# Scores of the first two batches with q as the stationary operand, in a TensorE-bound attention and gated-FFN kernel

## The chip, the cores and the metric

The kernel runs on one core of one Trainium2 chip. The metric is the device time of one execution in microseconds (us), the median of several runs. The engines are TensorE (PE: matmuls; its weight loads are shown as PEld), VectorE (DVE), ScalarE (ACT), GpSimd (POOL) and SyncE (SP, whose queue issues most of the transfers).

## The reference

```python
# q, k, v: (8 batches, 8 heads, 576 tokens, 64);  phi: (8, 8, 576, 32)
a = softmax(phi, over the 576 tokens)               # per memory slot
k_m = a.T @ k;  v_m = a.T @ v                       # 32 memory slots per head
attn = softmax(q @ k_m.T / 8, over the 32 slots)    # 576 x 32 per head
x = attn @ v_m                                      # heads side by side: 4608 x 512
out = (sigmoid(x @ w_gate) * (x @ w_val)) @ w_out   # 512 -> 1536 -> 512
```

All arrays are float32 to the caller. The weights come to the kernel in a form that it must convert to float32 on the chip.

## The kernel before, in words

The kernel never forms x. For each batch it multiplies v_m with the gate and value weights first (U: 32 slots of 8 heads by 256 columns for each of 12 blocks f of d_ff), and then U with the attention weights. Both operands are split into a high part and a rest (`at_hi`, `at_lo`, `u_hi`, `u_lo`), and each product is made of three matmuls (hi x hi, hi x lo, lo x hi). The same is done for the output product with `wo_hi`, `wo_lo`, `g_hi`, `g_lo`.

A step is one batch b and one block f, in two halves c of the tokens (0: the first 256; 1: the other 320, `CUT`). The first 20 steps, with all attention of batches 0 to 3 and part of batch 4's and all that is loaded and converted for them, are not planned by a loop but written out as a fixed list, `OPENING`. Each entry is an action; the entries of the list are issued in its order, so that on PE, DVE and ACT every engine works through its entries in that order, and on SP's queue the transfers stand in that order too. An engine whose next entry is not ready waits, whatever stands behind it. After the list, a loop does the other steps; it is not touched.

The actions that matter here (b is the batch, c the half of the tokens; for batches 2 and 3 mx, ms and hi, lo take both halves at once):

- `phi b`, `kvt b`, `kvm b g`, `q b c`, `gate f`, `out f`: transfers in. `more`, `keep`, `again`, `row`, `fetch`: further transfers (weights, spilled attention weights, partial outputs). The tiles ph, kvt, kvm0, kvm1 and q exist once each, so the next batch's transfer waits until the last reader is done.
- `sz`, `bc`, `bt` (gate weights) and `ws`, `wc`, `wb`, `wh`, `wl` (output weights): conversion, on ACT and DVE.
- `amax`, `aexp`, `T`, `A`, `Z`: the first softmax; T are PE transposes, A their copies out of PSUM. `K b g`, `B`, `t`, `V`: k_m and v_m, turned and kept.
- `S b c`: the scores. The 32 slots of a head are the stationary operand (64 rows x 32 columns), q is the moving one (`scores_of`), so slots lie on the partitions. `tr`: DVE transposes them in blocks of 32x32 out of PSUM into the tile e, tokens on partitions. `mx`, `ms`, `ex`, `nz`, `nm`: maximum, subtraction, exponential, sum and its reciprocal, product. `tn`: DVE transposes back. `hi`, `lo`: `at_hi` on ACT and `at_lo` on DVE.
- `U b f`: U for blocks f and f + 1 into two PSUM banks. `uh`: `u_hi` on ACT. `ul`: `u_lo`, on DVE the bank less `u_hi`. For (0, 0) and (0, 2), listed in `BY_PE`, `um` first has PE put minus `u_hi` into the banks and add the same sum once more, so that the bank holds the rest, and `ul` is a copy on ACT (`u_minus`, `u_rest`).
- `G b f c`: the 12 matmuls of gate and value; `sg`, `gm`, `gh`, `gl`: sigmoid, product and its split. `O b f c`: the six output matmuls; `E`, `row`: a partial or final row out.
- `W n`: n matmuls whose result nobody reads, put where PE would otherwise have nothing to do; another 24 stand ahead of the list.

PSUM has eight banks; until the first O, seven of them are handed out in turn (`bank`), and a bank is handed out again when its last reader is done.

Of the kernel before, what the change touches and what calls it, by code (L numbers as in the profile page):

```python
# [64 lines left out]
hi 1; gl 0 2 0; lo 1; O 0 2 0; sg 0 3 1; gh 0 2 1; gm 0 3 0; G 1 0 0; q 2 1; gm 0 3 1; gh 0 3 0; q 2 0;
gl 0 2 1; ws 3; kvm 3 0; gl 0 3 0; gh 0 3 1; keep 0; wc 3; G 1 0 1; sg 1 0 0; gl 0 3 1; sz 4; gm 1 0 0;
wb 3; sg 1 0 1; G 1 1 0; gh 1 0 0; amax 3; wh 3; O 0 2 1; sg 1 1 0; gm 1 0 1; gm 1 1 0; wl 3; S 2 0;
S 2 1; aexp 3; tr 2 0; O 0 3 0; tr 2 1; gl 1 0 0; mx 2; U 1 2; E 0 3 0 0; G 1 1 1; uh 1 2; ms 2;
E 0 3 0 1; gh 1 0 1; ul 1 2; O 0 3 1; row 0 3 1; row 0 3 0; ex 2; kvt 3; gl 1 0 1; G 1 2 0; more 1;
nz 2; O 1 0 0; sg 1 1 1; gh 1 1 0; gm 1 1 1; E 0 3 1 0; nm 2; G 1 2 1; E 0 3 1 1; sg 1 2 0; row 0 3 3;  # L70
gl 1 1 0; gm 1 2 0; O 1 0 1; bc 4; sg 1 2 1; gh 1 1 1; gm 1 2 1; U 2 0; tn 2; G 1 3 0; uh 2 0;
gl 1 1 1; hi 2; ul 2 0; O 1 1 0; gh 1 2 0; lo 2; gh 1 2 1; G 1 3 1; sg 1 3 0; sz 5; gl 1 2 1; q 3 1;
gm 1 3 0; q 3 0; gl 1 2 0; T 3 1; keep 1; Z 3; T 3 2; sg 1 3 1; O 1 1 1; A 3 1; gm 1 3 1; bc 5; T 3 0;
G 2 0 0; A 3 0; phi 4; row 0 3 2; A 3 2; gh 1 3 0; K 3 0; sg 2 0 0; gh 1 3 1; gm 2 0 0; gl 1 3 0; bt 4;
K 3 1; G 2 0 1; B 3; more 2; t 3; sg 2 0 1; G 2 1 0; V 3 0; gm 2 0 1; V 3 1; bt 5; O 1 2 0; S 3 0;
gh 2 0 0; gl 1 3 1; O 1 2 1; sg 2 1 0; tr 3 0; more 3; gm 2 1 0; gl 2 0 0; S 3 1; gh 2 0 1; U 2 2;
sz 6; tr 3 1; O 1 3 0; mx 3; uh 2 2; G 2 1 1; ul 2 2; E 1 3 0 0; gh 2 1 0; row 1 3 0; E 1 3 0 1; ms 3;
row 1 3 1; O 1 3 1; sg 2 1 1; keep 2; gm 2 1 1; gl 2 0 1; G 2 2 0; bc 6; ex 3; O 2 0 0; gl 2 1 0;
E 1 3 1 0; nz 3; E 1 3 1 1; G 2 2 1; gh 2 1 1; gl 2 1 1; nm 3; O 2 0 1; sg 2 2 0; sg 2 2 1; gm 2 2 0;
gm 2 2 1; G 2 3 0; tn 3; O 2 1 0; sg 2 3 0; ws 4; gm 2 3 0; amax 4; gh 2 2 0; G 2 3 1; gh 2 2 1; hi 3;  # L80
wc 4; gl 2 2 0; U 3 0; gh 2 3 0; gl 2 2 1; sg 2 3 1; gm 2 3 1; O 2 1 1; uh 3 0; lo 3; U 3 2; gl 2 3 0;
keep 3; ul 3 0; row 1 3 2; O 2 2 0; uh 3 2; row 1 3 3; ul 3 2; G 3 0 0; aexp 4; bt 6; O 2 2 1;
gh 2 3 1; G 3 0 1; more 4; O 2 3 0; sg 3 0 0; gm 3 0 0; wb 4; gh 3 0 0; G 3 1 0; E 2 3 0 0; sg 3 0 1;
row 2 3 0; gm 3 0 1; T 4 1; gl 2 3 1; G 3 1 1; A 4 1; sg 3 1 0; E 2 3 0 1; gm 3 1 0; gl 3 0 0;
gh 3 0 1; row 2 3 1; O 2 3 1; more 5; sg 3 1 1; kvm 4 1; gm 3 1 1; again 0; gl 3 0 1; U 0 4; E 2 3 1 0;
gh 3 1 0; G 3 2 0; uh 0 4; sz 7; ul 0 4; O 3 0 0; gh 3 1 1; bc 7; G 3 2 1; wh 4; E 2 3 1 1; wl 4;
sg 3 2 0; gm 3 2 0; O 3 0 1; gl 3 1 0; sg 3 2 1; gh 3 2 0; gm 3 2 1; G 3 3 0; ws 5; gh 3 2 1; gl 3 2 1;
O 3 1 0; gl 3 1 1; gl 3 2 0; sg 3 3 0; wc 5; G 3 3 1; wb 5; O 3 1 1; gm 3 3 0; sg 3 3 1; bt 7; wh 5;
gh 3 3 0; G 0 4 0; O 3 2 0; gl 3 3 0; more 6; sg 0 4 0; Z 4; kvm 4 0; gm 3 3 1; row 2 3 2; gm 0 4 0;
G 0 4 1; row 2 3 3; O 3 2 1; sg 0 4 1; gh 3 3 1; gm 0 4 1; more 7; U 0 6; G 0 5 0; uh 0 6; ul 0 6;  # L90
O 3 3 0; gl 3 3 1; G 0 5 1; wl 5; sg 0 5 0; gh 0 4 0; ws 6; E 3 3 0 0; wc 6; O 3 3 1; E 3 3 0 1;
row 3 3 0; gm 0 5 0; wb 6; row 3 3 1; G 0 6 0; gl 0 4 0; more 8; sg 0 5 1; O 0 4 0; gh 0 4 1; gm 0 5 1;
E 3 3 1 0; G 0 6 1; gh 0 5 0; E 3 3 1 1; gl 0 5 0; gl 0 4 1; gh 0 5 1; row 3 3 3; row 3 3 2; sg 0 6 0;
gl 0 5 1; O 0 4 1; wh 6; kvt 4; gm 0 6 0; sg 0 6 1; wl 6; gh 0 6 0; G 0 7 0; gm 0 6 1; ws 7; gl 0 6 0;
wc 7; O 0 5 0; sg 0 7 0; fetch 0 0; wb 7; gh 0 6 1; again 1; U 1 4; gl 0 6 1; wh 7; gm 0 7 0; O 0 5 1;
gh 0 7 0; sz 8; gl 0 7 0; wl 7; fetch 0 1; T 4 2; uh 1 4; O 0 6 0; ul 1 4; T 4 0; O 0 6 1; A 4 0;
A 4 2; O 0 7 0; G 0 7 1; E 0 7 0 0; E 0 7 0 1; row 0 7 0; row 0 7 1; K 4 0; sg 0 7 1; gm 0 7 1;
gh 0 7 1; K 4 1; gl 0 7 1; bc 8; fetch 0 2; U 1 6; B 4; uh 1 6; t 4; bt 8; O 0 7 1; V 4 0; V 4 1;
fetch 0 3; ul 1 6; E 0 7 1 0; E 0 7 1 1; row 0 7 3; row 0 7 2;
# [402 lines left out]

# [599 lines left out]
```

## Time and profile before

| | |
|---|---|
| median of 3 runs | 735.59 us (735.53 to 737.86) |
| the profiled execution | 736.14 us, span of its instructions 734.4 us |
| mean granted TensorE clock | 0.999 |
| PE busy | 724.2 us (99%), 5693 matmul records |
| PE weight loads busy | 607.7 us (83%) |
| DVE busy | 421.0 us (57%) |
| ACT busy | 337.6 us (46%) |
| DMA | 93.15 MB, mean 127 GB/s |

Times in the profile are microseconds from the span's first instruction. Busy time of PE includes the filler matmuls, and the end of a matmul is modelled: a matmul is shown for the whole of its way through the array, so that records overlap and the distance between the starts of two records tells the rate. A float32 matmul shows as two records, a transpose or a matmul of the split parts as one. A timeline row gives start, duration, engine, line of the kernel, operation, output and inputs, shape, how many records are merged in it (x), and in brackets how long the engine had been idle and what ended that. "64*32" is the part of the array in use, rows by columns; "64x256" is the moving operand.

### The profile page before, as it was taken

How to read it: one execution, taken by the hardware profiler on the slowest of the kernel's cores; microseconds unless marked ns; L12 is line 12 of the kernel's file. 1: busy time of each engine (PE TensorE's matmuls, PEld its weight loads, DVE VectorE, ACT ScalarE, POOL GpSimd, SP SyncE). 2: the span in 40 equal slices, each digit the busy share in tenths (PEclk: the TensorE clock that was granted, in tenths of full speed). 3: DMA queues.
4: the chain of work that ended last, by engine and by line, in shares of the span. 5: the costliest groups of instructions: out<-in, count | busy, mean ns of one | idle time of the engine just before them, and what ended most of it. 6: DMA issues, size and time to landing. Idle time of an engine off the chain costs nothing.

```text
span 734.4 us, 13802 instructions
## 1 busy us (share of the span) xinstructions
PE 724.2 (99%) x5693; PEld 607.7 (83%) x5693; DVE 421.0 (57%) x780; ACT 337.6 (46%) x787; POOL 4.5 (1%) x13
## 2 busy tenths in 40 slices
...
GB/s 364 358 285 195 207 279 168 237 172 226 273 342 160 243 150 80 132 165 15 148 238 58 2 94 147 29 30 65 1 1 59 1 0 15 1 58 1 1 1 71
DMA packets 29501, 93.15 MB, mean 127 GB/s; under 512 B 3328, under 2 KB 4352, under 8 KB 25856
## 3 DMA queue, kind: packets, MB, share of 16 engines
...
## 4 chain that ended last, share of the span: by engine, by line
PE 94%; DMA 4%; DVE 1%; SPq 0%; ACT 0%; issue 0%; POOL 0%; POOLq 0%; DVEq 0%; ACTq 0%
PE pu_t L186 55%; PE acc L186 39%; DMA kvm<-in_kvm_dram 2%; DMA q<-in_qT_dram 2%; DMA row<-part 1%; SPq L172 0%; DVE row L762 0%; DVE wg L280 0%; DVE e L509 0%; DVE e L524 0%; DVE mx L518 0%; DVE wo_raw L815 0%; ACT e L161 0%; ACT wo_raw L267 0%; ACT u_hi L627 0%
## 5 line engine op out<-in xcount | busy, mean ns | idle before, releaser
L186 PE MATMUL pu_t<-at_hi,u_hi 128*128 128x256 f32 (+1 forms) x764 | 227.7, 298 | 0.0
L186 PE MATMUL pu_t<-at_lo,u_hi 128*128 128x256 f32 (+1 forms) x764 | 224.4, 294 | 0.0
L186 PE MATMUL pu_t<-at_hi,u_lo 128*128 128x256 f32 (+1 forms) x764 | 224.0, 293 | 0.0
L711 DVE TENSOR_TENSOR sg<-pu_t,sg 128x256 f32<-128x256 f32 (+1 forms) x191 | 86.6, 455 | 160.2 <-ACT sg L161 98.3
L161 ACT ACTIVATE sg<-pu_t 128x256 f32<-128x256 f32 (+1 forms) x191 | 78.6, 412 | 194.7 <-PE pu_t L186 183.0
L186 PE MATMUL acc<-wo_hi,g_hi 128*128 128x512 f32 x384 | 154.6, 403 | 0.3 <-DVE row L762 0.3
L186 PEld LDWEIGHTS pu_t<-at_hi,u_hi 128*128 128x128 f32 x764 | 143.4, 188 | 11.7 <-issue 4.8
L186 PE MATMUL acc<-wo_hi,g_lo 128*128 128x512 f32 x384 | 151.1, 393 | 0.0
L186 PE MATMUL acc<-wo_lo,g_hi 128*128 128x512 f32 x384 | 150.6, 392 | 0.0
L186 PEld LDWEIGHTS pu_t<-at_lo,u_hi 128*128 128x128 f32 x764 | 143.4, 188 | 5.5
L186 PEld LDWEIGHTS pu_t<-at_hi,u_lo 128*128 128x128 f32 x764 | 143.2, 187 | 0.0
L722 ACT CAST g_hi<-sg 128x256 fp32r<-128x256 f32 x192 | 77.7, 406 | 109.0 <-DVE sg L711 96.3
L176 DVE TENSOR_TENSOR g_lo<-sg,g_hi 128x256 fp32r<-128x256 f32 x192 | 80.3, 420 | 61.8 <-ACT g_hi L722 61.7
L186 PEld LDWEIGHTS acc<-wo_hi,g_hi 128*128 128x128 f32 x384 | 72.0, 187 | 29.6 <-issue 19.0
L186 PEld LDWEIGHTS acc<-wo_hi,g_lo 128*128 128x128 f32 x384 | 72.1, 188 | 17.1
L186 PEld LDWEIGHTS acc<-wo_lo,g_hi 128*128 128x128 f32 x384 | 72.1, 188 | 9.4
L176 DVE TENSOR_TENSOR u_lo<-pu_t,u_hi 128x512 fp32r<-128x512 f32 x92 | 57.6, 684 | 27.5 <-ACT u_hi L627 27.5
L627 ACT CAST u_hi<-pu_t 128x512 fp32r<-128x512 f32 x95 | 49.4, 598 | 30.3 <-PE pu_t L186 30.0
L186 PE MATMUL pu_t<-wg,vT 64*32 64x512 f32 x784 | 50.8, 597 | 0.0
L186 PEld LDWEIGHTS pu_t<-wg,vT 64*32 64x32 f32 x784 | 11.9, 105 | 19.4 <-issue 17.0
L762 DVE TENSOR_TENSOR row<-acc,row 128x512 f32<-128x512 f32 x32 | 21.8, 688 | 6.8 <-DMA row<-part 3.7
L161 ACT ACT_TABLE_LOAD x18 | 23.1, 1283 | 1.0 <-PEq L1092 0.7
...
## 6 DMA issues: line engine op xcount, KB each, us to landing
...
```

What stands on the lines that cost most here:

```text
L161: last_act[0] = nc.scalar.activation(*args, **kw)
L176: return nc.vector.tensor_tensor(lo, x, hi.bitcast(F32), op=ALU.subtract)
L186: last_pe[0] = do(*args, **kw)
L627: nc.scalar.copy(U[b, fs[0]][0][:, r, :nf], pb[r])
L711: last_prod[0] = nc.vector.tensor_tensor(sg, val, sg, op=ALU.mult)
L722: nc.scalar.copy(ghi, prod[:, : 2 * P])
L762: nc.vector.tensor_tensor(st, o, st, op=ALU.add)
```

## The change

- The scores of batches 0 and 1 (`FLAT`) are made by `scores_flat`: q is the stationary operand (64 rows x 128 tokens), the 32 slots are the moving one. The result has tokens on the partitions at once, 256 columns to a bank, and a third bank takes the last 64 tokens of two heads' rows one under the other (`TAIL`).
- `tr` falls away for these batches. `flat_max` and `flat_minus` read the PSUM banks piece by piece (two pieces for c = 0, three for c = 1), and `flat_minus` writes e. For batch 1 they are done in two halves, too.
- `tn` is replaced by `tp`: PE turns the weights back, four transposes for c = 0 and five for c = 1, into PSUM; `hi` and `lo` read them there (`flat_hi`, `flat_lo`).
- `um`, `u_minus` and `u_rest` are gone; `ul` is DVE's subtraction everywhere. The tiles `minus` and `halves` are gone.
- The list `OPENING` is a new one, with the same actions otherwise. Some of what moved: phi 0 is first on SP's queue; kvm 1 0 and kvm 1 1 come after phi 2; K 1 0 and K 1 1 come after G 0 0 0; U 0 0 comes after tp 0 0; q 2 1 is ahead of kvm 2 1; kvm 4 1 comes late, after fetch 0 1; W 32 and W 16 stand around K 0 0.

```diff
+FLAT_CUT = {0: slice(0, 512), 1: slice(512, 2 * S), None: slice(0, 2 * S)}
...
+FLAT = (0, 1)
...
-BY_PE = [(0, 0), (0, 2)]
 OPENING = """
-out 0; gate 0; phi 0; kvt 0; gate 1; kvm 0 0; kvm 0 1; q 0 0; ws 0; wc 0; sz 0 0; sz 0 1; amax 0;
-bc 0 0; wb 0; aexp 0; bt 0 0; wh 0; W 65; T 0 0; bc 0 1; T 0 2; sz 1; T 0 1; wl 0; phi 1; A 0 2; q 0 1;
-bc 1; A 0 0; gate 3; A 0 1; W 14; K 0 0; Z 0; bt 1; kvm 1 0; W 3; K 0 1; B 0; bt 0 1; W 8; t 0; amax 1;
-V 0 0; V 0 1; W 4; S 0 0; tr 0 0; aexp 1; W 2; S 0 1; mx 0 0; U 0 0; ms 0 0; T 1 0; tr 0 1; ex 0 0;
-T 1 2; T 1 1; uh 0 0; nz 0 0; phi 2; kvt 1; sz 3; kvm 1 1; W 8; um 0 0; mx 0 1; gate 2; nm 0 0; out 1;
-A 1 2; q 1 0; A 1 1; ms 0 1; out 2; Z 1; q 1 1; ex 0 1; tn 0 0; nz 0 1; hi 0 0; A 1 0; amax 2; ul 0 0;
-W 27; K 1 0; nm 0 1; aexp 2; K 1 1; lo 0 0; tn 0 1; kvt 2; B 1; W 2; T 2 2; G 0 0 0; kvm 2 0; bc 3;
-out 3; hi 0 1; A 2 2; T 2 0; lo 0 1; sz 2; T 2 1; bt 3; G 0 0 1; phi 3; kvm 2 1; sg 0 0 0; t 1;
-G 0 1 0; bc 2; A 2 0; sg 0 0 1; A 2 1; gm 0 0 0; V 1 0; gm 0 0 1; W 2; G 0 1 1; gh 0 0 0; bt 2;
-gh 0 0 1; V 1 1; sg 0 1 0; ws 1; S 1 0; gl 0 0 0; W 2; U 0 2; gm 0 1 0; sg 0 1 1; tr 1 0; K 2 0;
-uh 0 2; gm 0 1 1; wc 1; gh 0 1 0; U 1 0; Z 2; wb 1; S 1 1; uh 1 0; um 0 2; tr 1 1; wh 1; wl 1; ul 0 2;
...
+phi 0; out 0; gate 0; gate 1; kvm 0 0; kvt 0; kvm 0 1; amax 0; ws 0; wc 0; wb 0; aexp 0; sz 0 1; W 33;
+T 0 0; T 0 1; wh 0; bc 0 1; T 0 2; A 0 2; phi 1; sz 1; bt 0 1; q 0 0; q 0 1; gate 2; A 0 0; bc 1;
+gate 3; A 0 1; sz 0 0; bc 0 0; W 32; K 0 0; bt 1; wl 0; W 16; K 0 1; Z 0; B 0; kvt 1; amax 1; W 8; t 0;
+bt 0 0; V 0 0; aexp 1; W 4; S 0 0; mx 0 0; S 0 1; ms 0 0; T 1 0; ex 0 0; mx 0 1; V 0 1; nz 0 0; W 7;
+T 1 2; T 1 1; A 1 1; phi 2; ms 0 1; kvm 1 0; kvm 1 1; nm 0 0; ex 0 1; q 1 0; Z 1; q 1 1; W 17; tp 0 0;
+A 1 0; nz 0 1; out 1; U 0 0; hi 0 0; lo 0 0; uh 0 0; nm 0 1; A 1 2; ul 0 0; W 12; tp 0 1; sz 2; amax 2;
+W 3; G 0 0 0; hi 0 1; sz 3; lo 0 1; aexp 2; W 4; K 1 0; bc 3; G 0 0 1; kvm 2 0; bc 2; bt 3; sg 0 0 0;
+K 1 1; sg 0 0 1; T 2 1; B 1; kvt 2; T 2 0; gm 0 0 0; t 1; gm 0 0 1; G 0 1 0; A 2 1; bt 2; V 1 0;
+gh 0 0 0; A 2 0; T 2 2; S 1 0; sg 0 1 0; V 1 1; mx 1 0; A 2 2; W 2; S 1 1; gh 0 0 1; gm 0 1 0; ms 1 0;
+U 0 2; q 2 1; kvm 2 1; mx 1 1; G 0 1 1; out 2; uh 0 2; phi 3; ms 1 1; gh 0 1 0; ws 1; gl 0 0 0; K 2 0;
+ul 0 2; sg 0 1 1; U 1 0; gl 0 0 1; wc 1; ex 1; G 0 2 0; gl 0 1 0; gm 0 1 1; Z 2; gh 0 1 1; wb 1;
...
 """
...
+    def scores_flat(b, c):
+        o = c * 512
+        pb = [bank(), bank()] + ([bank()] if c else [])
+        loaded[b, "pb", c] = [(pb[0], o, 256), (pb[1], o + 256, 256)] + ([(pb[2], 1024, P)] if c else [])
+        for u, nu in PIECES[c]:
+            at_u = u * NKT * 2 * P
+            qt = loaded[b, "q"][:, at_u : at_u + NKT * nu].rearrange("p (k n) -> p k n", k=NKT)
+            for i in range(max(nu // P, 1)):
+                for p in range(H):
+                    rs, l = of_head(b, 0, p)
+                    r, o = p % 2, p // 2 * M
+                    if nu == TAIL:
+                        matmul(pb[2][r * TAIL : (r + 1) * TAIL, o : o + M], qt[rs, p // 2, :], l, start=True, stop=True)
+                    else:
+                        o += i * P
+                        matmul(pb[r][:, o : o + M], qt[rs, p // 2, i * P : (i + 1) * P], l, start=True, stop=True)
+
+    def flat_max(b, c):
...
+        for pb, o, n in loaded[b, "pb", c]:
+            nc.vector.tensor_reduce(
+                mx[:, o // M : (o + n) // M], pb[:, :n].rearrange("p (w m) -> p w m", m=M), axis=AX.X, op=ALU.max
+            )
+
+    def flat_turn(b, c):
+        e = loaded[b, "e"]
+        pt = bank()
...
+        for r in range(2):
+            for i in range(2):
+                o = c * 512 + (2 * r + i) * P
+                transpose(pt[:, (2 * r + i) * P : (2 * r + i + 1) * P], e[:, o : o + P], ident)
+        if c:
+            pt = bank()
+            transpose(pt[:, :P], e[:, 1024 : 1024 + P], ident)
...
+    def flat_hi(b, c):
...
+        for pt, cs in loaded[b, "at", c]:
+            nc.scalar.copy(at[b][0][:, :, cs], pt)
...
-    def u_minus(b, fs):
-        pb, hi = loaded[b, "u", fs[0]], U[b, fs[0]][0]
-        for r in range(2):
-            matmul(pb[r], minus, hi[:, r, : len(fs)], start=True, stop=False)
-        u_sum(b, fs, pb, False)
-
-    def u_rest(b, fs):
...
-            last_u[0] = nc.scalar.copy(lo[:, r, :nf], pb[r])
```

More of the change, by code (lines that the diff above doesn't have):

```diff
@@ L65 @@
[L65 to L99, printed above, removed]
+phi 0; out 0; gate 0; gate 1; kvm 0 0; kvt 0; kvm 0 1; amax 0; ws 0; wc 0; wb 0; aexp 0; sz 0 1; W 33;
@@ new lines @@
+G 0 2 1; nz 1; more 0; sg 0 2 0; K 2 1; sg 0 2 1; wh 1; uh 1 0; G 0 3 0; gm 0 2 0; kvm 3 1; gm 0 2 1;
+q 2 0; gl 0 1 1; out 3; B 2; nm 1; O 0 0 0; kvt 3; kvm 3 0; wl 1; tp 1 0; gh 0 2 0; ul 1 0; O 0 0 1;
+hi 1 0; sg 0 3 0; ws 2; gl 0 2 0; G 0 3 1; amax 3; gh 0 2 1; gl 0 2 1; O 0 1 0; lo 1 0; sg 0 3 1;
+gm 0 3 0; gm 0 3 1; t 2; wc 2; tp 1 1; V 2 0; gh 0 3 0; wb 2; G 1 0 0; hi 1 1; V 2 1; lo 1 1; O 0 1 1;
+sg 1 0 0; wh 2; gm 1 0 0; gl 0 3 0; wl 2; S 2 0; S 2 1; tr 2 0; ws 3; O 0 2 0; wc 3; wb 3; aexp 3;
@@ new lines @@
+U 1 2; tr 2 1; O 0 2 1; wh 3; mx 2; gh 0 3 1; G 1 0 1; uh 1 2; wl 3; ms 2; gh 1 0 0; O 0 3 0; gl 0 3 1;
+ex 2; ul 1 2; O 0 3 1; E 0 3 0 0; gl 1 0 0; E 0 3 0 1; G 1 1 0; nz 2; row 0 3 1; row 0 3 0; O 1 0 0;
+keep 0; sg 1 0 1; Z 3; sg 1 1 0; gm 1 0 1; nm 2; gh 1 0 1; T 3 2; G 1 1 1; A 3 2; sz 4; gm 1 1 0; tn 2;
+T 3 0; gh 1 1 0; G 1 2 0; sg 1 1 1; gm 1 1 1; A 3 0; gl 1 0 1; E 0 3 1 0; T 3 1; gh 1 1 1; G 1 2 1;
+row 0 3 2; more 1; E 0 3 1 1; gl 1 1 1; gl 1 1 0; sg 1 2 0; row 0 3 3; gm 1 2 0; O 1 0 1; bc 4;
@@ new lines @@
+sg 1 2 1; A 3 1; hi 2; gm 1 2 1; K 3 0; gh 1 2 0; lo 2; U 2 0; bt 4; K 3 1; q 3 0; uh 2 0; keep 2;
+q 3 1; G 1 3 0; B 3; sz 5; ul 2 0; more 2; O 1 1 0; gh 1 2 1; sg 1 3 0; G 1 3 1; gm 1 3 0; gl 1 2 0;
+bc 5; O 1 1 1; sg 1 3 1; gh 1 3 0; gl 1 3 0; G 2 0 0; gm 1 3 1; bt 5; t 3; G 2 0 1; V 3 0; V 3 1;
+gh 1 3 1; gl 1 2 1; sg 2 0 0; O 1 2 0; gm 2 0 0; sg 2 0 1; sz 6; more 3; gm 2 0 1; keep 1; gl 1 3 1;
+S 3 0; kvt 4; O 1 2 1; tr 3 0; bc 6; S 3 1; U 2 2; tr 3 1; O 1 3 0; bt 6; uh 2 2; gh 2 0 0; G 2 1 0;
@@ new lines @@
+E 1 3 0 0; E 1 3 0 1; row 1 3 0; gl 2 0 0; ul 2 2; O 1 3 1; row 1 3 1; sg 2 1 0; phi 4; ws 4; gh 2 0 1;
+gm 2 1 0; G 2 1 1; mx 3; gh 2 1 0; ms 3; E 1 3 1 0; O 2 0 0; sg 2 1 1; row 1 3 2; E 1 3 1 1; gm 2 1 1;
+G 2 2 0; row 1 3 3; gl 2 1 0; gl 2 0 1; more 4; amax 4; kvm 4 0; O 2 0 1; sg 2 2 0; gh 2 1 1; gl 2 1 1;
+U 3 0; gm 2 2 0; wc 4; ex 3; O 2 1 0; gh 2 2 0; nz 3; G 2 2 1; uh 3 0; aexp 4; ul 3 0; O 2 1 1;
+gl 2 2 0; G 2 3 0; nm 3; sg 2 2 1; gm 2 2 1; O 2 2 0; tn 3; gh 2 2 1; sg 2 3 0; G 2 3 1; gl 2 2 1;
@@ new lines @@
+hi 3; gm 2 3 0; gh 2 3 0; lo 3; O 2 2 1; sg 2 3 1; gl 2 3 0; G 3 0 0; gm 2 3 1; Z 4; gh 2 3 1; O 2 3 0;
+sg 3 0 0; gm 3 0 0; gh 3 0 0; G 3 0 1; gl 3 0 0; E 2 3 0 0; gl 2 3 1; E 2 3 0 1; wb 4; O 2 3 1;
+sg 3 0 1; more 5; gm 3 0 1; row 2 3 0; gh 3 0 1; G 3 1 0; row 2 3 1; again 0; U 3 2; sg 3 1 0; wh 4;
+gm 3 1 0; gh 3 1 0; G 3 1 1; uh 3 2; ul 3 2; E 2 3 1 0; O 3 0 0; sg 3 1 1; sz 7; gm 3 1 1; gl 3 0 1;
+G 3 2 0; E 2 3 1 1; bc 7; row 2 3 3; row 2 3 2; U 0 4; sg 3 2 0; gm 3 2 0; gl 3 1 0; uh 0 4; G 3 2 1;
```

61 lines of the change are left out of this document (42 added, 19 removed).

## The prediction

> **What bounds the kernel now.** I read the page's busy times first, then a table of four stretches, then TensorE's timeline.
>
> ```profile
> PE 724.2 (99%) x5693; PEld 607.7 (83%) x5693; DVE 421.0 (57%) x780; ACT 337.6 (46%) x787; POOL 4.5 (1%) x13
> 0.00:36.00 36.00, 31.95 (x423) 24.30 (x423) 26.51 (x49) 19.84 (x41) 0.69 (x6) 1.00 0.92 360
> 36.00:60.00 24.00, 23.11 (x291) 18.41 (x290) 21.33 (x35) 18.66 (x36) 0.00 (x0) 1.00 0.77 306
> 60.00:187.00 127.00, 127.00 (x1057) 105.28 (x1057) 98.30 (x172) 79.19 (x177) 0.00 (x0) 1.00 0.57 204
> 187.00:734.00 547.00, 542.10 (x3929) 459.75 (x3927) 274.85 (x526) 219.90 (x535) 3.84 (x7) 1.00 0.25 86
> ```
>
> The columns are stretch, length, then busy PE, weight loads, DVE, ACT, POOL, granted clock, DMA share, GB/s. From 60 to 187 us PE is busy 127.00 of 127.00 us: it is the bound there, and what it executes there is the same set in both lists. So the change is worth what it does to two things: the moment X at which the first gate product G 0 0 0 starts, and the PE work between X and the end of the list (first at_hi,u_hi product of step 20, at 187.08). Before X much of PE's "busy" is filler matmuls; DVE (26.51 of 36) and DMA (share 0.92) decide.
>
> ```profile
> 17.95 1.08 PE L186 MATMUL pu_t<-kvm,e 128*32 128x128 f32 x32
> 21.26 0.67 PE L186 MATMUL acc<-q,kT 64*32 64x256 f32 x16
> 22.18 0.77 PE L186 MATMUL pu_t<-q,kT 64*32 64x256 f32 x32
> 22.75 1.22 PE L186 MATMUL pu_t<-wg,vT 64*32 64x512 f32 x16
> 23.91 1.21 PE L186 MATMUL acc<-ident,ph 128*128 128x128 f32 x9
> 27.51 3.12 PE L186 MATMUL acc<-ident 128*128 128x256 bf16 x27
> 34.45 1.08 PE L186 MATMUL pu_t<-kvm,left 128*32 128x128 f32 x32 [2.58 <-DMA kvm<-in_kvm_dram]
> 35.68 0.39 PE L186 MATMUL acc<-ident 128*128 128x256 bf16 x2
> 35.94 0.36 PE L186 MATMUL pu_t<-at_hi,u_hi 128*128 128x256 f32 x1
> 187.08 0.28 PE L186 MATMUL pu_t<-at_hi,u_hi 128*128 128x256 f32 x1
> ```
>
> X is 35.94 now. The last thing ahead of it is K 1 1 (34.45), which stood 2.58 us for its kvm transfer.
>
> **The price of a flat score.** Each matmul shows as two records (16 for the 8 heads of S 0 0). New: c=0 has 16 matmuls, so 32 loads of 128 columns of q and 32 matmuls that stream only 32 columns; c=1 has 24, of which 8 (the tail) load 64 columns. The loads bind, not the streams. The trace has no 64x128 load; the nearest rows:
>
> ```profile
> 206.80 1.95 PE L186 MATMUL pu_t<-wg,vT 64*32 64x512 f32 x32
> 208.68 0.51 PE L186 MATMUL acc<-wo_hi,g_hi 128*128 128x512 f32 x1
> 209.02 0.40 PE L186 MATMUL acc<-wo_lo,g_hi 128*128 128x512 f32 x1
> 209.26 0.39 PE L186 MATMUL acc<-wo_hi,g_lo 128*128 128x512 f32 x1
> L186 PE MATMUL pu_t<-q,kT 64*32 64x64 f32 x48 | 1.0, 216 | 0.0
> ```
>
> After narrow tiles the first wide product is followed at 0.34 us instead of 0.23-0.24: an exposed 128-column load is 0.11. Nine transposes take 1.21, that is 8 steps of 0.117 or a little less with the 0.27 of one: 0.109 a step. I take 0.11 a load. The 32 U matmuls take 1.88 us though one lasts 0.6: eight tiles (two row halves, four column groups) run side by side. Heads alternate between the row halves, so I let the two halves load side by side: c=0 is 16 rounds, 16 x 0.11 + 0.2 of fill = 1.95; c=1 is 16 x 0.11 + 8 x 0.055 + 0.2 = 2.4. The last row (48 records of 64 columns, three runs, 1.0 us: 0.33 each, of which 0.216 is one record) gives 0.055 for a round of eight 32-column loads, so loads do overlap, but this is as well explained by four column groups side by side with the row halves in turn. Ends: rounds of 0.055 (as that row) and halves in turn, 0.22. I take 0.11 because wide loads resemble the wide rows.
>
> [...]
>
> **X in the new list.** phi goes first on SP's queue, but the bytes ahead of kvm 0 1 are the same ones in another order, and DMA is full; K 0 1 (17.95) does not move, nor do B, t, V behind it: S 0 0 stays at 21.26. W 32 and W 16 fill the wait. kvm 1 0 and 1 1 now follow phi 2; K 1 no longer stands ahead of G 0 0 0, so their lateness is covered until about 36. The chain then:
>
> ```profile
> 22.09 0.78 DVE L509 STREAM_TRANSPOSE e<-acc 128x256 f32<-128x256 f32 x2 [0.33 <-PE acc L186]
> 22.91 0.69 DVE L518 TENSOR_REDUCE mx<-e 128x16 f32<-128x512 f32 x1
> 24.24 0.91 DVE L509 STREAM_TRANSPOSE e<-pu_t 128x320 f32<-128x320 f32 x2
> 25.08 0.69 DVE L540 TENSOR_REDUCE zs<-e 128x16 f32<-128x512 f32 x1
> 26.01 0.25 DVE L542 RECIPROCAL zs<-zs 128x16 f32<-128x16 f32 x1
> 26.86 0.68 DVE L548 TENSOR_TENSOR e<-e,zs 128x512 f32<-128x512 f32 x1
> 28.46 0.75 DVE L572 STREAM_TRANSPOSE u_hi<-e 128x256 f32<-128x256 f32 x2
> 29.25 0.62 ACT L579 CAST at_hi<-u_hi 128x512 fp32r<-128x512 f32 x1 [0.21 <-DVE u_hi L572]
> 31.57 0.81 DVE L548 TENSOR_TENSOR e<-e,zs 128x640 f32<-128x640 f32 x1
> 45.23 0.42 DVE L711 TENSOR_TENSOR sg<-pu_t,sg 128x256 f32<-128x256 f32 x1
> 50.80 1.28 DVE L176 TENSOR_TENSOR u_lo<-pu_t,u_hi 128x512 fp32r<-128x512 f32 x2
> ```
>
> The transposes tr (0.78, 0.91) and tn (0.75, and as much for c=1) leave DVE. mx and ms now read PSUM in pieces of 256; a 256-wide PSUM read is 0.42, two pieces about 0.76, the three of c=1 about 0.95. Bounds for such a reduce: no dearer than the transposes from PSUM (0.46 a piece), no cheaper than half of 0.69; 0.42 is the nearest in size and source. Step by step: S 0 0 ends 23.3; mx 24.1; ms 24.9; S 0 1 ends 25.5 and its mx, queued ahead of nz 0 0 on DVE, 26.45; nz 0 0 (25.08 to 26.26 now: 1.2) 27.6; ms 0 1 28.6; nm 0 0 29.3; tp 0 0, four transposes, 30.05; hi 30.75; lo 31.5; nm 0 1 (0.81) 32.4 (U 0 0 and uh 0 0 run beside, done 32.3); ul 0 0 (two pieces, 1.28, formerly ACT's through the second sum) 33.7. tp 0 1 and W 3 fit beside ul. **X = 33.8**, 2.1 us earlier. PE alone, from 21.26: 1.95 + 2.3 (S) + 1.0 (T) + 24 x 0.11 (W) + 0.5 (tp) + 1.0 (U) + 1.3 (W 12) + 0.6 + 0.3 = 32.9; that is the low end. High end: PSUM reads at the transposes' price and 0.1 more at each handover, 34.6.
>
> **PE work behind X**, new less old:
>
> ```profile
> 44.01 0.66 PE L186 MATMUL acc<-q,kT 64*32 64x256 f32 x16
> 44.61 0.39 PE L186 MATMUL acc<-ident 128*128 128x256 bf16 x2
> 48.27 0.75 PE L186 MATMUL acc<-q,kT 64*32 64x256 f32 x32
> 48.95 0.50 PE L186 MATMUL acc<-u_hi,minus 128*128 128x512 f32 x1
> 51.55 1.08 PE L186 MATMUL pu_t<-kvm,left 128*32 128x128 f32 x32 [0.85 <-DMA kvm<-in_kvm_dram]
> ```
>
> Row by row:
>
> - K 1 0, K 1 1, moved behind X: 2 x 1.23 (34.45 to 35.68) = +2.46.
> - um 0 2 gone, with the stall that followed it: 51.55 - 48.95 = -2.60. (um 0 0 was ahead of X, where filler takes its place.)
> - S 1: 1.95 + 2.4 against 0.60 + 0.68 = +3.07.
> - tp 1: nine transposes at 0.11 and two fills of 0.1 = +1.19.
> - T 2 2 moved behind X, two more W: +0.33.
>
> Sum +4.45; with X, **4.45 - 2.14 = +2.3 us**. ACT loses the two halves of u_rest twice, off the path. DVE loses tr 1 and tn 1 and gains ul 0 2 (1.28), time nobody waits for unless a bank does: PE's G 0 1 0 (41.4) takes the bank that gm 0 0 0 releases, and that stands on DVE behind amax 2, lo 0 1, bc 3, bc 2 and bt 3.
>
> ```profile
> 30.36 1.29 DVE L364 TENSOR_REDUCE nmx<-ph 128x2 f32<-128x1152 f32 x1
> 38.04 1.22 DVE L280 SCALAR_TENSOR_TENSOR wg<-wg 128x1024 int32<-128x1024 int32 x1
> 41.16 0.70 DVE L273 TENSOR_SCALAR wg<-wg 128x1024 int32<-128x1024 int32 x1
> ```
>
> From 33.7: 1.3 + 0.9 + two bc of 2 x 0.70 + two steps of 1.22 for bt 3 = 41.2, gm 41.6: just in time; if it slips, PE slips. q 2 1 stands ahead of kvm 2 1 on SP's queue and waits until S 1 1 has read the only q tile (47.5); about 1.7 MB at the stretch's 306 GB/s land near 54, K 2 1 comes at 56: covered by 2 us, and without it a stall like the 0.85 above. kvm 4 1 is moved past two fetches; three O halves (6 x 0.23 each), a G and K 4 0 stand between its issue and K 4 1, some 7 us. I charge nothing for these, and 1.5 us to the high side.
>
> The profiled execution took 736.14 (span 734.4), 0.55 above the median of the three runs; so 738.4 for such an execution, 737.9 for the median. I say 738.0. About 0.3% (2.2 us) is what a measurement of this kernel can tell from no change.
>
> **Rivals.**
> 1. Row halves load in turn (rounds of 0.22). S 0 0 ends 1.7 later, S 0 1 3.8, and nz 0 0 is queued behind it: X 37.5; S 1 costs 3.8 more. +2.3 + 7.6 = +9.9: 745.5. For it: nothing in the trace has two 64-row halves loading wide at once; against: eight tiles do run at once.
> 2. The other side: a half's load is half as dear, rounds of 0.055 as in the 64-column row. Each batch has 36 equivalents of a round on the path (16 + 16 + 8 halves), 72 in all: -72 x 0.055 = -4.0, so -1.7: 733.9. It decides from a round of 0.078 down (no loss), and a gain over 0.3% needs 0.048. Against it: all wide rows stand at 0.11.
> 3. A load waits for the matmul of its own row half: rounds of 0.11 + 0.028 (half of a 64-column stream's 0.055): 72 x 0.028 = 2.0, +4.3: 739.9. Against it: wide products follow each other at 0.23 with their 0.11 load wholly hidden. [...]
> 4. The new list meets a bank or transfer stall between 36 and 66, where DVE was already busy 21.33 of 24: +1.5 to +4 on top, 740 to 742.
>
> **Numbers.** Forecast as worked out 0.50 (its own range 736.4 to 739.5, from X at 32.9 and 34.6, and a little for stalls); rival 1 0.15; rival 2 0.15; rival 3 0.07; rival 4 0.13. The range 734.5 to 745.0 leaves out the lower part of rival 2 and the upper of rival 1, under 0.2 together. Slower by over 0.3% (above 737.8): 0.24 of the forecast and rivals 1, 3 and 4, 0.59. Same: the other 0.26 of the forecast and 0.07 of rival 2, 0.33. Faster: 0.08, the part of rival 2 with rounds below 0.048.
>
> **What would show it.** PE's first at_hi,u_hi product at 33 to 34.6 (late: rival 1; 32: rival 2); the flat scores' records 1.9 and 2.4 us long in sum, and the spacing of equal row halves 0.11; no wait on kvm ahead of K 1 1; PE 127 of 127 from 60 on; the first product of step 20 near 189.4. I am wrong if the 64x128 loads are priced otherwise, or if DVE's chain from S 0 0 to ul 0 0 is not 12.4 us long.

## The result, and the profile after

The changed kernel takes 742.96 us (median of 4 runs, 742.91 to 742.99) beside 735.99 for the kernel before (median of 4): ratio 1.0083, 95% interval 1.0071 to 1.0095. It is slower by 7.0 us, where 738.0 and +2.3 had been forecast: the sign and the range held, the size did not. The profiled execution took 742.91 (span 741.0), so its rows stand for the median.

The page's busy times, and the same three stretches as before (columns as there):

```profile
PE 732.0 (99%) x5740; PEld 617.3 (83%) x5740; DVE 419.8 (57%) x788; ACT 333.0 (45%) x783; POOL 4.6 (1%) x13
0.00:36.00 36.00, 32.37 (x365) 27.08 (x366) 23.31 (x47) 16.24 (x33) 1.38 (x7) 0.95 0.84 331
36.00:60.00 24.00, 23.89 (x321) 19.35 (x321) 20.54 (x39) 16.23 (x33) 0.00 (x0) 0.93 0.74 278
60.00:187.00 127.00, 127.00 (x1014) 105.87 (x1013) 98.07 (x174) 76.60 (x174) 0.55 (x1) 1.00 0.62 222
```

From 60 us on PE is again busy 127.00 of 127.00. Ahead of that two columns are new: the granted clock is 0.95 and 0.93, where it was 1.00 in both, and POOL has worked 1.38 us instead of 0.69. TensorE's timeline:

```profile
19.25 1.08 PE L187 MATMUL pu_t<-kvm,e 128*32 128x128 f32 x32 [1.22 <-DMA kvm<-in_kvm_dram]
...
22.56 1.98 PE L187 MATMUL acc<-kT,q 64*128 64x32 f32 x32
24.37 2.88 PE L187 MATMUL pu_t<-kT,q 64*128 64x32 f32 x48
...
28.09 1.70 PE L187 MATMUL acc<-ident 128*128 128x256 bf16 x7
...
35.76 0.36 PE L187 MATMUL acc<-at_hi,u_hi 128*128 128x256 f32 x1
...
50.33 1.96 PE L187 MATMUL acc<-wg,vT 64*32 64x512 f32 x16
...
193.85 0.28 PE L187 MATMUL pu_t<-at_hi,u_hi 128*128 128x256 f32 x1
```

Step 20's first product stands at 193.85 instead of 187.08: +6.77, the whole change. Of it X (the first gate product) gives -0.18 (35.76 against 35.94, forecast 33.8), and the work behind X 6.95 (forecast 4.45). Three of these rows are out of the forecast. K 0 1 stands 1.22 us for its kvm and starts at 19.25 instead of 17.95. Seven filler products (28.09) take 1.70 us, where 27 took 3.12. And the U product at 50.33 takes 1.96, where 16 such records took 1.22.

What is new ahead of that kvm transfer is in POOL's timeline, first of before and then of after:

```profile
187.98 0.67 POOL L172 DMA_DIRECT2D words<-in_wo_dram  x1 [186.68 <-DVE u_lo L176]
```

```profile
1.27 0.66 POOL L173 DMA_DIRECT2D words<-in_wo_dram  x1 [0.33 <-issue]
```

A 512 KB transfer of wo that belongs to the loop behind the list goes out at 1.27 us, as it waits for nothing now. The diff does not touch it. The slow products are explained by the clock, microsecond by microsecond (each row ends with granted clock, DMA share and GB/s):

```profile
26.00:27.00 1.00, 1.00 (x22) 0.96 (x20) 0.65 (x2) 0.89 (x2) 0.00 (x0) 0.69 0.80 301
27.00:28.00 1.00, 1.00 (x10) 0.94 (x8) 0.82 (x3) 0.00 (x0) 0.00 (x0) 0.50 0.12 33
28.00:29.00 1.00, 1.00 (x7) 0.67 (x6) 0.93 (x5) 0.00 (x0) 0.00 (x0) 0.50 0.05 18
29.00:30.00 1.00, 1.00 (x7) 0.87 (x6) 1.00 (x4) 0.00 (x0) 0.00 (x0) 0.61 0.00 0
50.00:51.00 1.00, 1.00 (x22) 0.51 (x26) 1.00 (x4) 0.00 (x0) 0.00 (x0) 0.63 0.00 0
51.00:52.00 1.00, 1.00 (x16) 0.00 (x0) 0.99 (x4) 0.00 (x0) 0.00 (x0) 0.50 0.77 86
52.00:53.00 1.00, 1.00 (x11) 0.79 (x4) 0.01 (x1) 0.62 (x2) 0.00 (x0) 0.50 0.84 307
53.00:54.00 1.00, 1.00 (x6) 1.00 (x5) 1.00 (x2) 1.00 (x3) 0.00 (x0) 0.66 0.66 241
```

Twice the clock is halved. What is missing from 1.00 sums to 1.70 and 1.71 us, so it was halved for 3.4 us each time: in windows of 0.1 us from 26.38 to 29.79, the end of the flat scores of batch 0 and what follows them, and from 50.27 to 53.68, as those of batch 1 end. PE is busy 1.00 in every one of these rows.

### The profile page after: what moved, and what is told of

Same layout as the page of the kernel before. It is cut to its first block, busy times and chain, and to the rows that moved or that the text cites. A ratio compares the mean times of both kernels' runs of the same rounds, so it can differ in the third digit from the quotient of the medians.

```text
span 741.0 us, 13914 instructions
## 1 busy us (share of the span) xinstructions
PE 732.0 (99%) x5740; PEld 617.3 (83%) x5740; DVE 419.8 (57%) x788; ACT 333.0 (45%) x783; POOL 4.6 (1%) x13
## 4 chain that ended last, share of the span: by engine, by line
PE 94%; DMA 2%; DVE 2%; ACT 0%; SPq 0%; issue 0%; DVEq 0%; ACTq 0%
PE pu_t L187 56%; PE acc L187 39%; DMA kvm<-in_kvm_dram 2%; SPq L173 0%; DVE wg L281 0%; DVE wg L273 0%; DVE wg L274 0%; DVE row L811 0%; DVE u_lo L177 0%; DVE nmx L365 0%; ACT wg L256 0%; ACT wg L268 0%; DVE sg L760 0%; ACT at_hi L560 0%; DVE e L612 0%
## 5 line engine op out<-in xcount | busy, mean ns | idle before, releaser
L187 PE MATMUL pu_t<-at_hi,u_hi 128*128 128x320 f32 (+1 forms) x748 | 223.1, 298 | 0.0
L187 PE MATMUL pu_t<-at_lo,u_hi 128*128 128x320 f32 (+1 forms) x748 | 219.7, 294 | 0.0
L187 PE MATMUL pu_t<-at_hi,u_lo 128*128 128x320 f32 (+1 forms) x748 | 219.4, 293 | 0.0
L760 DVE TENSOR_TENSOR sg<-pu_t,sg 128x320 f32<-128x320 f32 (+1 forms) x188 | 85.6, 456 | 163.7 <-ACT sg L162 103.8
L162 ACT ACTIVATE sg<-pu_t 128x256 f32<-128x256 f32 (+1 forms) x186 | 76.4, 412 | 189.5 <-PE pu_t L187 185.0
L187 PEld LDWEIGHTS pu_t<-at_hi,u_hi 128*128 128x128 f32 x748 | 140.4, 188 | 11.1 <-issue 3.5
L187 PEld LDWEIGHTS pu_t<-at_lo,u_hi 128*128 128x128 f32 x748 | 140.4, 188 | 5.3
L187 PEld LDWEIGHTS pu_t<-at_hi,u_lo 128*128 128x128 f32 x748 | 140.2, 187 | 0.0
L187 PE MATMUL pu_t<-wg,vT 64*32 64x512 f32 x752 | 47.4, 597 | 0.0
L187 PE MATMUL acc<-ident 128*128 128x256 bf16 x162 | 22.0, 294 | 2.4 <-POOL ident masks.py:199 2.4
```

Of the source, the lines that this page charges most:

```text
L162: last_act[0] = nc.scalar.activation(*args, **kw)
L187: last_pe[0] = do(*args, **kw)
L760: last_prod[0] = nc.vector.tensor_tensor(sg, val, sg, op=ALU.mult)
```

## The experiments

Two theories came from this. A: taking out the `minus` tile (512 bytes a partition) moved the memory of the early pool, so that the late `words` tile depends on nothing and its transfer goes ahead of kvm 0 1. B: the flat scores stream little for the time that they take, and the clock is granted by what is streamed. Times are medians; each ratio is to the kernel before, run beside it. Behind step 20 the profiled executions take 549.1 to 551.0 us, though the loop there is the same, so differences of about 1 us are read at step 20's first product and not from the times.

**e1, a dead tile in the place of `minus`.**

```diff
+    pools["conv"].tile([P, P], F32R, name="minus", bufs=1)
     warm(24)
```

> The changed kernel plus one unused 512-byte-per-partition tile in the pool of the early words, where the -1 matrix stood; nothing is computed with it. Theory A: taking that tile out moved the addresses, so that the first `words` transfer of wo (512 KB, POOL's queue) lost the waits that held it until 188 us and now goes out at 1.27 us, ahead of the first batch's bytes. With the tile back it goes out near 188 again; PE's first product stands at 1.36 instead of 2.38, kvm 0 1 lands at 17.8 instead of 19.1, K 0 1 starts at 17.95 instead of 19.25, G 0 0 0 at 34.4 instead of 35.76, and the whole is 1.3 us shorter: about 741.7, ratio to the kernel before 1.0065. Rival: SP's queue is the limit whatever POOL moves, K 0 1 stays at 19.25 and the time at 743.

Measured: 742.29, ratio 1.0071 (1.0049 to 1.0092). POOL, the first stretch and PE:

```profile
193.06 0.67 POOL L173 DMA_DIRECT2D words<-in_wo_dram  x1 [191.75 <-DVE u_lo L177]
```

```profile
0.00:36.00 36.00, 34.51 (x360) 28.55 (x361) 22.81 (x46) 15.75 (x33) 0.70 (x6) 0.91 0.78 312
```

```profile
18.16 1.08 PE L187 MATMUL pu_t<-kvm,e 128*32 128x128 f32 x32
...
23.28 3.89 PE L187 MATMUL pu_t<-kT,q 64*128 64x32 f32 x48
...
36.26 0.36 PE L187 MATMUL acc<-at_hi,u_hi 128*128 128x256 f32 x1
...
192.82 0.28 PE L187 MATMUL pu_t<-at_hi,u_hi 128*128 128x256 f32 x1
```

The transfer is late again and K 0 1 is 1.09 earlier, as A says. But X is not: 36.26. The clock of the first stretch fell to 0.91, twice the loss, and S 0 1 lasts 3.89 us; from 36 to 60 us it is 1.00. So the halved time is the same 6.8 us as in the change, all of it ahead of X here, and step 20 stands 1.03 earlier (192.82 against 193.85). That is A's price with the clock's loss unchanged; the ratios (1.0071 against 1.0083) go the same way, but their intervals overlap.

**e2, fillers between the flat scores.**

```diff
                     else:
                         ...
+                    if r:
+                        matmul(idle[:, :256], spare[:, :P], spare, start=True, stop=True)
```

> The changed kernel with one bf16 filler product (128x256, 0.109 us) after every second head of a flat score: 20 for each of batches 0 and 1, none elsewhere. Theory B: the granted clock fell to 0.5 for 3.41 us twice because the flat scores stream little (27 of each 109 ns) while their loads take the time. With fillers both stretches stay at 1.00, U 0 2 takes 1.1 us instead of 1.89 and G 0 1 1 1.93 instead of 2.61. The fillers cost 0.9 in S 0 0 and 1.3+0.9 in S 1, so the sum is the 2.3 us that the clock gives back against 3.1: 743 to 744.5, the same as without. Rival: the clock falls for another reason (a fixed time, the load of the other engines); then the half-clock stretches stay, U 0 2 still takes 1.9 and the time is 746.

Measured: 764.25, ratio 1.0368 (1.0344 to 1.0392). Neither theory's number. PE of batch 0:

```profile
22.71 0.41 PE L187 MATMUL acc<-kT,q 64*128 64x32 f32 x4
23.05 0.28 PE L187 MATMUL acc<-ident 128*128 128x256 bf16 x1
23.27 0.41 PE L187 MATMUL acc<-kT,q 64*128 64x32 f32 x4
```

Two heads and a filler take 0.56 us (22.71 to 23.27) where two heads took 0.23 (an eighth of S 0 0's 1.81): a filler of 0.109 costs 0.33, so the change from 64-row to 128-row products and back costs 0.22. What 32 columns stream is an estimate: in the kernel before, 512-column products of the same kind start 0.45 us behind each other in one part of the array (49.61 to 50.06), which makes 0.027 to 0.028 for 32. So the fillers hardly raised the streamed share, from 27 of 112 ns (24%) to 0.163 of 0.56 us (the filler's 0.109 and two rounds of 0.027: 29%), and made the scores last more than twice as long; the clock fell further (0.88 in the first 36 us, against 0.95; with 0.90 from 36 to 60 us and 0.86 from 60 to 110, what is missing from 1.00 makes an estimated 13.4 us of halved clock ahead of 60 us and 14.0 behind, where the change had 3.4 twice). It doesn't speak against B, but it isn't the test that it was meant to be.

**e3, four heads of one row half, then four of the other.**

```diff
-                for p in range(H):
+                for p in (0, 2, 4, 6, 1, 3, 5, 7):
```

> The changed kernel with the heads of a flat score in the order 0 2 4 6 1 3 5 7, four of one row half and then four of the other. Theory: a round cost 0.109 us because the loads of the two row halves run side by side. Then each half's four heads load one after the other, S 0 0 takes 3.5 us instead of 1.81, S 0 1, S 1 0 and S 1 1 grow alike (72 rounds of 0.11 in all, 7.9 us at most), and the whole takes 747 to 751. Rival: a load of 64 rows is simply half as dear as one of 128 rows, whichever half it goes to; then S 0 0 stays at 1.8 and the time at 743.

Measured: 746.78, ratio 1.0135 (1.0102 to 1.0169). S 1 0 on PE, of after and of this run (`acc` is one row half's bank, `pu_t` the other's):

```profile
45.61 0.29 PE L187 MATMUL acc<-kT,q 64*128 64x32 f32 x1
45.62 0.29 PE L187 MATMUL pu_t<-kT,q 64*128 64x32 f32 x1
45.74 0.27 PE L187 MATMUL acc<-kT,q 64*128 64x32 f32 x1
45.75 0.27 PE L187 MATMUL pu_t<-kT,q 64*128 64x32 f32 x1
45.85 0.27 PE L187 MATMUL acc<-kT,q 64*128 64x32 f32 x1
```

```profile
46.61 0.74 PE L187 MATMUL acc<-kT,q 64*128 64x32 f32 x5
47.09 0.29 PE L187 MATMUL pu_t<-kT,q 64*128 64x32 f32 x1
47.19 0.27 PE L187 MATMUL acc<-kT,q 64*128 64x32 f32 x1
47.22 0.27 PE L187 MATMUL pu_t<-kT,q 64*128 64x32 f32 x1
```

After: both halves start 0.01 apart, a pair every 0.11. Here five records of one half, alone, spread over 46.61 to 47.08 (0.74 less the 0.27 of one, four gaps of 0.12). So a 64-row load costs 0.12 here, as much as the 0.11 that the prediction read off the 128-row ones, and alternating halves hide one behind the other (a pair every 0.11). The rival (half as dear) falls. S 1 0 takes 2.43 us (46.61 to 49.04) instead of 1.91, not twice as long, because PE takes up the other half after four records of the first and the two run side by side from there on. The rise of the whole, 3.8 us by the ratios, is not the loads' alone: behind batch 1 the clock is halved for 6.8 us instead of 3.4 (0.86 instead of 0.93 from 36 to 60 us), an estimated 1.7 us of it.

**e4, the kernel before without um 0 2.**

```diff
-BY_PE = [(0, 0), (0, 2)]
+BY_PE = [(0, 0)]
-... uh 1 0; um 0 2; tr 1 1; ...
+... uh 1 0; tr 1 1; ...
```

> The kernel before with the second sum of U 0 2 alone taken out (um 0 2; its remainder is subtracted on DVE as in the change), the list otherwise as it was. The prediction booked -2.60 us for this edit. Theory: in the old list PE stands for the kvm of K 2 right behind it until that transfer lands, so 1.75 us of the 2.60 only lengthen that stall and step 20's first product comes at about 186.9 to 187.1 (before: 187.08), time 735.5 to 736. Rival (the prediction's term): 184.5, time 733.4.

Measured: 737.58, ratio 1.0013 (1.0001 to 1.0025; the profiled execution took 736.57); step 20's first product at 186.97. K 2 0 and K 2 1:

```profile
45.98 1.08 PE L186 MATMUL pu_t<-kvm,left 128*32 128x128 f32 x32 [0.95 <-DVE wo_raw L272]
51.02 1.08 PE L186 MATMUL pu_t<-kvm,left 128*32 128x128 f32 x32 [2.18 <-DMA kvm<-in_kvm_dram]
```

The stall ahead of K 2 1 grew from 0.85 to 2.18 and a new one of 0.95 came ahead of K 2 0. In the old list the second sum filled a wait; alone, its removal is worth nothing.

**e5, each flat score streams its columns twice** (with e1's tile; the second copy falls on columns that a later head overwrites or that nobody reads; the tail's products likewise).

```diff
-matmul(pb[r][:, o : o + M], qt[...], l, start=True, stop=True)
+matmul(pb[r][:, o : o + 2 * M].rearrange("p (n m) -> p n m", m=M), qt[...],
+       l.unsqueeze(1).broadcast_to([D, 2, M]), start=True, stop=True)
```

> The dead-tile kernel with every product of a flat score streaming its 32 columns twice (the second copy lands in columns that a later head overwrites): loads, order and banks as before, only the streamed share of a round doubles from 27 to 54 of 112 ns. Theory B: the granted clock follows what TensorE streams, not how busy it is. Then S 0 0 and S 1 0 still take 1.8 to 1.9 us (the loads bind), but the half-clock stretches behind them go or shrink: S 0 1 2.4 instead of 3.8, G 0 0 0 at 34.4 to 34.8 instead of 36.26, step 20's first product at 191.0 to 191.5, time 741. Rival: the clock falls whatever is streamed; S 0 1 stays at 3.8 and the time at 742.3.

Measured: 739.38, ratio 1.0031 (1.0020 to 1.0042). The first stretch, and PE:

```profile
0.00:36.00 36.00, 34.61 (x411) 28.80 (x415) 25.52 (x50) 18.84 (x37) 0.70 (x6) 1.00 0.87 346
```

```profile
21.48 2.00 PE L187 MATMUL acc<-kT,q 64*128 64x64 f32 x32
23.31 2.56 PE L187 MATMUL pu_t<-kT,q 64*128 64x64 f32 x48
...
26.30 0.93 PE L187 MATMUL acc<-ident 128*128 128x256 bf16 x7
...
33.13 0.36 PE L187 MATMUL acc<-at_hi,u_hi 128*128 128x256 f32 x1
...
47.74 1.09 PE L187 MATMUL acc<-wg,vT 64*32 64x512 f32 x16
...
189.73 0.28 PE L187 MATMUL pu_t<-at_hi,u_hi 128*128 128x256 f32 x1
```

Doubling what is streamed makes the kernel faster: the clock holds (1.00 in all three stretches), S 0 0 lasts as long as before (21.48 to 23.31), S 0 1 2.56 instead of e1's 3.89, seven fillers 0.93 instead of 1.70, and U 0 2 1.09, where the change took 1.96. All runs agree: the mean clock of an execution was 0.980 to 0.997 in the 16 of after, e1, e2 and e3, and 0.998 or more in the 35 of the versions that stream twice or four times (e5, e6, e10, e11, e12); the kernel before lay at 0.993 to 1.000, so the mean alone would not settle it, and the rows do. B stands. The forecast of X is even outdone (33.13 against 34.4 to 34.8 expected here, 33.8 in the prediction).

**e6, four times.** The same edit with 4 for 2.

> The same with the 32 columns streamed four times: a record streams about 107 ns beside a load of 112. Theory B: full clock. For the loads: if the load of a row half runs while that half's own product streams, rounds stay at 0.11 to 0.12, S 0 0 at 1.8 to 2.0 and the time at 741. Rival (the prediction's third): a load waits for the product of its own half; rounds become 0.22, S 0 0 3.5 us, and the time 746 to 748. At 32 columns the two differ by only 27 ns a round, here by 107.

Measured: 740.43, ratio 1.0046 (1.0030 to 1.0063); clock 1.00 in all three stretches.

```profile
21.38 2.06 PE L187 MATMUL acc<-kT,q 64*128 64x128 f32 x32
23.27 2.97 PE L187 MATMUL pu_t<-kT,q 64*128 64x128 f32 x48
```

S 0 0 takes 1.89 us (21.38 to 23.27), 0.118 a round, while each half streams an estimated 107 to 112 ns of it (four times 0.027 to 0.028): a half's load runs beside its own stream. The prediction's third rival would want 0.22 with four copies and falls.

**e7, batch 1 on the old score path**, in the new list (its turned scores in a tile of the early pool, which also holds `words` back).

```diff
-FLAT = (0, 1)
+FLAT = (0,)
-... mx 1 0; ... ms 1 0; ... mx 1 1; ... ms 1 1; ... tp 1 0; ... tp 1 1; ...
+... tr 1 0; ...             tr 1 1; mx 1; ... ms 1; ... tn 1 0; ... tn 1 1; ...
```

> The new list with batch 0 as in the change and batch 1 on the old path (tokens on the columns; DVE's transposes tr 1 and tn 1 in place of the first max and of tp 1; its turned scores in a tile of their own in the early pool, which also brings the late `words` back to 188 us). The prediction booked S 1 at +3.07 and tp 1 at +1.19. Theory: PE is the bound behind G 0 0 0, so 4.26 comes off: step 20's first product at 188.6 (dead tile alone: 192.8), no half-clock stretch at 50, time 738. Rival: DVE, which gets 3.4 us of transposes back, or a bank that it holds makes PE wait; then 190 to 191 and 740.

Measured: 738.63, ratio 1.0023 (1.0010 to 1.0036); step 20 at 189.17. The clock was 0.95 ahead of 36 us and 1.00 behind, so the halved stretch behind batch 1 goes with batch 1's being flat. X was 34.64, and behind it the list took 154.53, 2.1 less than e5's 156.60, not 4.26: U 0 2 and S 2 1 now stand 0.38 and 0.73 us for DVE. The truth lies between the two theories.

**e8, the list alone**: both batches on the old path, in e7's manner.

> The new list, without the second sum, with both batches on the old score path: what the list and U do without the flat scores. Theory: PE's work behind G 0 0 0 is that of before plus K 1 (2.46) less um (2.60) plus 0.33, near zero; G 0 0 0 starts at 34.8 to 35.5, by DVE's chain with the transposes in it; the clock stays at 1.00 in both stretches; step 20's first product at 187 to 188, time 736.5 to 737.5, the same as before. Then the loss of the change is the flat scores' own. Rival: the list itself loses (late transfers, DVE); 190 or more, 739 to 740.

Measured: 737.92, ratio 1.0012 (1.0001 to 1.0022).

```profile
31.52 0.39 PE L187 MATMUL acc<-at_hi,u_hi 128*128 128x256 f32 x1 [0.68 <-ACT tails L394]
...
32.56 0.39 PE L187 MATMUL acc<-at_hi,u_lo 128*128 128x256 f32 x1 [0.54 <-DVE u_lo L177]
...
187.68 0.28 PE L187 MATMUL pu_t<-at_hi,u_hi 128*128 128x256 f32 x1
```

X comes at 31.52 and stops once more for u_lo until 32.56. That is earlier than expected, and earlier than with flat scores (33.13): the list and the dropped second sum bring X forward, the flat form does not.

**e9 and e10, K 1 into the fillers' place**, in e8 and in e5; K 1 0 for W 12, K 1 1 behind G 0 0 0 without W 4, its kvm ahead of phi 2, gm 0 0 0 ahead of bt 3, A 1 2 earlier; in e9 U 0 2 goes behind G 0 1 1, too.

```diff
-... ul 0 0; W 12; ... W 3; G 0 0 0; ... W 4; K 1 0; bc 3; G 0 0 1; ... bt 3; ... K 1 1; ...
+... ul 0 0; K 1 0; ... W 3; G 0 0 0; ... K 1 1; bc 3; G 0 0 1; ... gm 0 0 0; gm 0 0 1; bt 3; ...
```

> The list-alone kernel (old score path for both batches) reordered: kvm 1 0 and kvm 1 1 ahead of phi 2 on SP's queue, where DMA stood half idle (24 to 28 us); K 1 0 in the place of 12 filler products ahead of G 0 0 0, K 1 1 between G 0 0 0 and G 0 0 1 without the 4 fillers there; gm 0 0 0 and gm 0 0 1 ahead of bt 3 on DVE; U 0 2 behind G 0 1 1, ul 0 2 ahead of ms 1. Theory: PE loses 1.23+0.54 us of work behind G 0 0 0 and the 0.69 us wait for the bank of G 0 1 0; step 20's first product at 185.5 instead of 187.7, time 735.5 to 736.5, a little under the kernel before. Rival: DVE binds between 30 and 60 us (busy 23.6 of 24) and what PE saves comes back as waits; 187.5 and 738.

> The change with the dead tile and the streams doubled, and the same reordering of K 1, kvm 1, gm 0 0 0 and gm 0 0 1 (U 0 2 stays where it is). Theory: G 0 0 0 stays at 33.1 (DVE's chain sets it), and PE's work behind it falls by 1.23+0.54 and the 0.4 us wait ahead of t 1: step 20's first product at 187.9 to 188.4 instead of 189.7, time 737.5 to 738, still not faster than before, because S 1 costs PE 3.2 us more than the old scores. Rival: the moved work meets a wait (kvm 1 lands late, phi 2 late for amax 2): 189.5 to 190.5, 739 to 740.

Measured: 737.86, ratio 1.0012 (1.0003 to 1.0021), and 739.92, ratio 1.0040 (1.0028 to 1.0053): nothing gained (step 20 at 188.35 against e8's 187.68, and at 189.39 against e5's 189.73). In e9, PE's moved work turned into waits, for a transfer, ACT and DVE; the longest is 1.93 us ahead of G 0 2 0. In e10 the moved kvm made phi 2 late for amax 2:

```profile
34.13 1.35 DVE L365 TENSOR_REDUCE nmx<-ph 128x2 f32<-128x1152 f32 x1 [0.97 <-DMA ph<-in_phiT_dram]
```

Its followers (lo 0 1, the exponentials, the sigmoids) shift with it, and G 0 1 0 waits 0.91 us. Both rivals came true in kind.

**e11, streamed twice and no dead tile**: the changed kernel with e5's edit alone.

> The changed kernel with the streams of the flat scores doubled and nothing else: the dead tile is left out, so the 512 KB of late `words` go out at 1.27 us again. Against the run with both (G 0 0 0 at 33.13, step 20 at 189.73, 739.4) it prices the early transfer by itself, with the clock held. Theory A: K 0 1 starts at 19.25 instead of 18.16, G 0 0 0 at 34.2 to 34.4, step 20's first product at 190.8 to 191.0, time 740.5 to 740.7. Rival: the 1.1 us are taken up by DVE's slack behind S 0 0; 33.2, 189.8 and 739.4.

Measured: 740.14, ratio 1.0044 (1.0032 to 1.0056).

```profile
19.02 1.08 PE L187 MATMUL pu_t<-kvm,e 128*32 128x128 f32 x32 [0.68 <-DMA kvm<-in_kvm_dram]
...
33.98 0.36 PE L187 MATMUL acc<-at_hi,u_hi 128*128 128x256 f32 x1
...
190.67 0.28 PE L187 MATMUL pu_t<-at_hi,u_hi 128*128 128x256 f32 x1
```

Against e5: K 0 1 0.86 later, X 0.85, step 20 0.94. That is A's price with the clock held, near the 1.03 of e1. Against the change: step 20 at 190.67 instead of 193.85, 3.18 us for the clock alone.

**e12, streamed twice, batch 0 flat only.**

> Batch 0 flat with the streams doubled, batch 1 on the old path, with the dead space that keeps `words` late: between the list alone (187.7, 737.9) and both batches flat (189.7, 739.4), all at full clock. Theory: G 0 0 0 at 33.1 as with both flat, and behind it the 154.5 us of the run with batch 0 flat alone: step 20's first product at 187.6, time 737.8 to 738.0; so the flat form of batch 0 costs nothing against the list alone and the 1.5 us are batch 1's. Rival: each batch costs half, 188.7 and 738.7.

Measured: 737.16, ratio 1.0004 (0.9996 to 1.0013); X 33.04, and step 20:

```profile
188.09 0.28 PE L187 MATMUL pu_t<-at_hi,u_hi 128*128 128x256 f32 x1
```

So batch 0's flat form is worth nothing that can be told against the list alone (step 20 0.41 later, the medians the other way), and batch 1's costs 1.64 at step 20 (189.73 against 188.09). No version ran faster than the kernel before; this one's time equals it, though step 20 stands 1.01 later than in the trace of before.

## Why the prediction was right in sign and short in size

The 6.77 us at step 20, against the forecast's +2.3:

| part | forecast | measured | from |
|---|---|---|---|
| X, clock and transfers as forecast | -2.14 | -2.81 | e5: 33.13 |
| work behind X, the same | +4.45 | +5.46 | e5: 189.73 - 33.13, less 187.08 - 35.94 |
| `words` ahead of kvm 0 1 | 0 | +0.94 | e11 less e5 |
| clock halved twice | 0 | +3.18 | after less e11 |

The first two make +2.65, and e5's time is 1.0031 of before, where the forecast was 738.0 over 735.59, 1.0033. In sum the steps that were worked out held, in part because their misses cancel: X came 0.67 better than forecast, the work behind it 1.01 worse. Two that had been left at nothing did not hold. The clock rows fit the last line: they lack 3.41 us in all, and 3.18 of it arrives at step 20.

- **"The bytes ahead of kvm 0 1 are the same ones in another order"** failed. I counted SP's queue, which the list orders, and not POOL's. Its transfer of the loop was held only by what shared its memory. That the tile's absence frees it is shown (e1, e11); that the cause is the address is argued.
- **"The loads bind, not the streams"** was right, and its other half was missed: an engine that waits for its loads also streams little (an estimated 27 of 112 ns here). The forecast took the clock as 1.00 throughout, from a trace in which no work of this kind stood.
- **The price of a flat score** held: a round 0.11; S 0 0 1.81 (1.95 forecast), S 1 1 2.49 (2.4). No row shows the sums' 0.2 of fill as a term of its own: 16 rounds of 0.113 make the whole 1.81. Rivals 1 and 2 fall by e3's and after's spacing, rival 3 by e6.
- **X** was right by its number and half wrong by its reason. The sum took the transposes off DVE and called the result 2.1 us; e8 keeps them and has X at 31.52 to 32.56. What brings X forward is the list: K 1 1's wait of 2.58 no longer stands ahead of it (e9 and e10 put K 1 0 ahead again, and X stays at 31.82 and 32.94), nor does the second sum, whose share there was not tried alone. The flat products give back on PE (1.2 us for S 0 0 alone) what DVE saves. DVE's chain from S 0 0 to ul 0 0, put at 12.4, took 11.9 in e5 (21.48 to 33.34) and 13.4 in the change (22.56 to 35.96), with the clock's loss in it.
- **Behind X**, in e5: K 1 +2.46 and um 0 2 with its stall -2.60, as forecast. That -2.60 needs the new list, in which K 2 1 finds its kvm landed; in the old one it is worth nothing (e4). S 1 gives +3.20 (3.07). tp 1 is smaller than its +1.19: PE is at it for 0.82 (two stretches of 0.355 and 0.465). T 2 2 and the fillers give +0.49 (0.33). Not listed at all: t 1 waits for B 1, 0.75 against 0.36, and half a dozen first products behind another form cost about 0.1 each (X is followed at 0.21, the product after it at 0.11).
- **Rival 4** (a bank or transfer stall, 740 to 742) comes nearest in number and not in mechanism: G 0 1 0 finds its bank at 41.27 in e5 (forecast 41.6), K 2 1 and K 4 1 stand for no transfer, and PE is busy 23.89 of 24. None of the four rivals was the clock.
